# A banded convolution and soft mixture of experts on one core: convolutions and channel turns as two 64-row tiles

## The chip, the cores and the metric

The kernel runs on one core of a Trainium2 chip, in one launch. The metric is the device time of that launch in microseconds (us), measured three times before the change. A profile of one more execution gives the durations and waits used below. The engines are called as in the profile: PE (TensorE, the matrix engine; PEld are its weight loads), DVE (VectorE), ACT (ScalarE), POOL (GpSimd) and SP (SyncE, which here only starts DMAs).

## What is computed

A causal convolution over seven positions, whose taps are a softmax of `weight_gen`, one set for each token and head; then a soft mixture of experts over all 28672 tokens. All is float32.

```python
w = softmax(weight_gen, axis=-1)                     # (8, 3584, 8 heads, 7 taps)
out = einsum('bshk,bskhg->bshg', w, x_unf)           # x_unf: 7 shifted copies of x
x = out.reshape(28672, 192)
logits = x @ phi                                     # 32 slots
d = softmax over the tokens (axis 0) of logits
slot_input = (d.T @ x).reshape(8, 4, 192)            # 8 experts, 4 slots each
h = maximum(slot_input[e] @ w1[e], 0); slot_out[e] = h @ w2[e]
c = softmax over the slots (axis 1) of logits
return c @ slot_out
```

## The kernel before

**Tiling.** A group is 104 tokens: four blocks of 26. A batch has 35 groups, so there are 280 groups, 140 pairs and 70 slots of two pairs. `x` comes by supergroups of five groups into a ring `xbd` (a view of `big`): the rows of a block's 32 positions, four times on the partitions, once for each of four heads, in block-diagonal form, so that one contraction over 128 partitions does four heads at once. The off-diagonal parts are zeroed once (`clear`, L354) and only the diagonal is loaded (`loadx`, L152, four DMAs of 120 KB).

**Taps.** A chunk is 8 groups of taps, one chunk for two slots, 35 in all. A chunk goes through `tap_top` (DVE maximum), `tap_sub` (POOL), `tap_exp` (ACT), `tap_sum` (three folds on POOL), `tap_inv` (DVE reciprocal), `tap_mul` (POOL, writes the taps on diagonals of `wide`) and `tap_turn` (DVE transpose of 32 by 32 blocks), which gives a `band`, the stationary operand of the convolution.

**Loop.** For each pair, `conv` (L222) does 16 matmuls: 2 groups, 2 halves of the heads, 4 blocks, each of 128 rows by 26 weight columns with 96 columns streamed, into one PSUM bank `cv`, the block choosing the 32 partitions written. `conv_out` (L235) copies 384 columns to `tm` on ACT. `xpose` (L241) turns a pair's channels to the partitions with three transposes of 122 rows by 128 columns into `pt`, and `xpose_out` (L252) copies 312 columns to `cm` on ACT. For every unit of 8 pairs (four slots), `logits` (L271) multiplies by `phi`, `top`, `newmax`, `newmax_out`, `dexp`, `dturn` keep a running maximum over the tokens and its exponentials, and `dispatch` (L334) adds `d.T @ x`; `fade` and `rescale` correct the sum for a new maximum. `soft` (L75) does the row softmax `c` of a half batch in seven steps over DVE, POOL and ACT; the first 13 (`EARLY`) of 16 halves run inside the loop.

**Order.** The queues are filled in an order that the program works out: every piece is an `op` with its engine, an assumed cost, what it reads and writes and sometimes a due time, and `model` places them. PE and SP keep the order in which the loop writes them; DVE, ACT and POOL are sorted. In a slot, PE does two `conv`, with `newmax` between them where it is due, then `logits` where due, two `xpose`, and `dispatch` where due.

**Rings before the change.** Four `x` buffers of four zeroed quarter heads, four `taps`, one `wide`, three `band`, two `tm`, four `cv` (a bank each), two `pt` (a bank each), one bank each for the logits `ls` and the accumulator `acb`. After the loop, the experts' network runs on `accS` (the accumulated sum), and the output is 49 evictions from PSUM into parts of `big` and as many DMAs.

Of the kernel before, what the change touches and what calls it, by code (L numbers as in the profile page):

```python
# [42 lines left out]
def conv_soft_moe(ctx, tc, xh, wh, phi, w1a, w1b, w2, out):  # L43
# [96 lines left out]
    A.copy(xbd[:, 0, 2], zero.to_broadcast([128, NBC * GW]))  # L140
    V.memset(xbd[:, 0, 3], 0.0)
    for t in taps:
        V.memset(t[:, :, KT], EPS)
# [19 lines left out]
    def seven(t):  # L163
        return t.rearrange("p b k j -> p b j k")

    def each(t, n):
        return t.unsqueeze(2).to_broadcast([128, n, KT, T])

    def tap_top(c, b=ALL):
        n = b.stop - b.start  # L170
        m = tops[c, b.start] = pa.tile([128, CH, T], F32, tag="top", name=f"top{c}_{b.start}")[:, 0:n]
        V.tensor_reduce(out=m, in_=seven(taps[c % NTAP][:, b, 0:KT]), axis=AX.X, op=ALU.max)  # L172
# [6 lines left out]
    def tap_exp(c, b=ALL):  # L179
        t = taps[c % NTAP][:, b, 0:KT]  # L180
        A.activation(t, t, AF.Exp)  # L181

    def tap_sum(c, b=ALL, eng=None):
        n = b.stop - b.start
        m = tsums[c, b.start] = pa.tile([128, CH, T], F32, tag="sum", name=f"sum{c}_{b.start}")[:, 0:n]
        t, s = taps[c % NTAP][:, b], fold[:, b]
        if eng is None:
            V.tensor_reduce(out=m, in_=seven(t), axis=AX.X, op=ALU.add)
            return
        eng.tensor_tensor(out=s, in0=t[:, :, 0:4], in1=t[:, :, 4:8], op=ALU.add)  # L190
        eng.tensor_tensor(out=s[:, :, 0:2], in0=s[:, :, 0:2], in1=s[:, :, 2:4], op=ALU.add)
        eng.tensor_tensor(out=m, in0=s[:, :, 0], in1=s[:, :, 1], op=ALU.add)  # L192
# [5 lines left out]
    def tap_mul(c, b=ALL, eng=G):  # L198
# [3 lines left out]
        w = wide[:, b]  # L202
        dst = bass.AP(w.tensor, w.offset, [w.ap[0], [T * 32, n], [1, KT], [33, T]])
        eng.tensor_tensor(out=dst, in0=taps[c % NTAP][:, b, 0:KT],  # L204
                          in1=each(m, n), op=ALU.mult)

    def tap_turn(c, b=ALL):

        V.transpose(bands[c % NBAND][:, b].rearrange("p b j l -> p (b j l)"),  # L209
                    wide[:, b].rearrange("p b j -> p (b j)"))  # L210
# [11 lines left out]
    def conv(p):  # L222
        cv = cvs[p % NCV]
        for par in range(2):
            g = 2 * p + par
            t = g // SGG
            for c in range(2):
                for blk in range(4):
                    o = 4 * GW * (2 * par + (c ^ par))
                    i, b = ((4 * (g % m) + blk) * 2 + c for m in (4, SGG))  # L230
                    P.matmul(cv[32 * blk : 32 * blk + T, o : o + 4 * GW],  # L231
                             bands[g // 8 % NBAND][:, g // 4 % CH, :, i],
                             xbd[:, t % NXS, :, b * GW : (b + 1) * GW], start=True, stop=True)

    def conv_out(p, copy=A.copy):  # L235
        u, pr = unit(p)
        copy(tms[u % NTM][:, pr, 1 : 2 * D + 1], cvs[p % NCV][:, 0 : 2 * D])  # L237
# [3 lines left out]
    def xpose(p):  # L241
        u, pr = unit(p)
# [3 lines left out]
        pt = ps_t.tile([128, 4, 128], F32, tag="pt", name=f"pt{p}")[:, 0:3]  # L246
        pts[p] = pt
        for i in range(3):
            P.transpose(pt[:, i, 0:TR], tm[0:TR, pr, 1 + 128 * i : 129 + 128 * i],  # L249
                        ident[0:TR, 0:TR])  # L250

    def xpose_out(p, copy=A.copy):  # L252
        u, pr = unit(p)
        copy(cms[u][:, pr].rearrange("p i b j -> p (i b) j"),  # L254
             pts.pop(p).rearrange("p i (b j) -> p (i b) j", j=32)[:, :, 0:T])

# [46 lines left out]
    def newmax_out(u):  # L303
        negm[u] = pa.tile([128, 1], F32, tag="nm", name=f"nm{u}", bufs=3)
        V.tensor_reduce(out=negm[u], in_=pm[:, 0 : 4 + (u > 0)], axis=AX.X, op=ALU.min)
# [27 lines left out]
    def dispatch(u, lo=0, hi=2 * UP):  # L333
# [3 lines left out]
        if lo == 0:  # L337
            acs[u] = (acb if u < final else cvs[sum(UNITS[u]) % NCV])[:, 0 : D + 1]
# [571 lines left out]
```

## Time and profile before

| | us |
|---|---|
| median of 3 runs | 321.17 (320.27 to 323.70) |
| the profiled execution | 320.73 |
| its span, first to last instruction | 319.0 |
| mean granted clock of PE | 0.925 |
| PE busy | 272.7 |
| DVE busy | 220.8 |
| ACT busy | 185.5 |
| POOL busy | 154.7 |
| DMA, 70.06 MB | 220 GB/s over the span |

An engine's busy time is the sum of its instructions, over stages with different limits: an opening without steady work for PE, the loop, the experts' network, and an output stage in which PE has little to do. Float32 matmuls show as two records each (2240 matmuls of the convolution, 4480 records), transposes as one. In a row of the timeline, the first two numbers are the start and the length from the first record's start to the last one's end, and xN counts the records merged; the bracket at the end is idle time of that engine and what ended it.

### The profile page before, as it was taken

How to read it: one execution, taken by the hardware profiler on the slowest of the kernel's cores; microseconds unless marked ns; L12 is line 12 of the kernel's file. 1: busy time of each engine (PE TensorE's matmuls, PEld its weight loads, DVE VectorE, ACT ScalarE, POOL GpSimd, SP SyncE). 2: the span in 40 equal slices, each digit the busy share in tenths (PEclk: the TensorE clock that was granted, in tenths of full speed). 3: DMA queues.
4: the chain of work that ended last, by engine and by line, in shares of the span. 5: the costliest groups of instructions: out<-in, count | busy, mean ns of one | idle time of the engine just before them, and what ended most of it. 6: DMA issues, size and time to landing. Idle time of an engine off the chain costs nothing.

```text
span 319.0 us, 15477 instructions
## 1 busy us (share of the span) xinstructions
PE 272.7 (85%) x6816; PEld 210.1 (66%) x6816; DVE 220.8 (69%) x366; ACT 185.5 (58%) x425; POOL 154.7 (49%) x236
## 2 busy tenths in 40 slices
PE   6656999999999999999999999999989987789100
PEld 6645888788788888887888887878768721223000
DVE  5826669788688787788796895797436689964200
ACT  5553666777678677687677667676642266534200
POOL 5867553756857757687639665486015500000000
PEclk9587999999999999999999999999999999985555
DMA  5267467758765767677667756763990069999994
GB/s 169 57 176 217 134 196 212 209 165 234 182 208 159 217 187 209 184 225 201 193 188 211 221 162 190 206 189 85 392 386 8 4 233 402 400 400 402 400 401 172
DMA packets 32146, 70.06 MB, mean 220 GB/s; under 512 B 5456, under 2 KB 14800, under 8 KB 32080
## 3 DMA queue, kind: packets, MB, share of 16 engines
q1 hardware_dynamic: 32080, 69.08, 67.7%
q8 instruction: 53, 0.87, 1.2%
q14 instruction: 13, 0.11, 0.1%
HBM read 46.70 MB, written 22.36 MB: 217 GB/s over the span
## 4 chain that ended last, share of the span: by engine, by line
PE 62%; DMA 13%; DVE 10%; POOL 4%; issue 3%; ACT 2%; SPq 0%; ACTq 0%; DVEq 0%; POOLq 0%
PE cv L231 28%; PE pt L249 14%; DMA out<-big 8%; PE ls L278 7%; PE acb L342 7%; DMA taps<-wh 5%; DVE band L209 2%; DVE big L808 2%; PE hpb L732 2%; PE so L753 2%; DVE top L172 1%; POOL big L358 1%; DVE cT L445 1%; POOL wide L204 1%; ACT big L808 1%
## 5 line engine op out<-in xcount | busy, mean ns | idle before, releaser
L231 PE MATMUL cv<-big,band 128*26 128x96 f32 x4480 | 117.5, 255 | 10.8 <-POOL si L190 4.4
L231 PEld LDWEIGHTS cv<-big,band 128*26 128x26 f32 x4480 | 103.3, 132 | 22.2 <-issue 9.5
L237 ACT COPY tm<-cv 128x384 f32<-128x384 f32 x140 | 67.2, 482 | 43.0 <-PE cv L231 40.0
L209 DVE STREAM_TRANSPOSE band<-wide 128x1664 f32<-128x1664 f32 (+1 forms) x37 | 66.6, 1801 | 3.4 <-POOL wide L204 3.3
L254 ACT COPY cm<-pt 128x312 f32<-128x312 f32 x140 | 53.9, 424 | 18.4 <-PE pt L249 18.3
L249 PE MATMUL pt<-ident,tm 122*128 122x122 f32 x420 | 60.0, 279 | 2.7 <-ACT cm L254 2.7
L249 PEld LDWEIGHTS pt<-ident,tm 122*128 122x128 f32 x420 | 43.8, 142 | 15.4 <-issue 5.8
L176 POOL TENSOR_TENSOR taps<-taps,top 128x364 f32<-128x364 f32 (+1 forms) x35 | 31.1, 892 | 29.0 <-DVE top L172 29.0
L204 POOL TENSOR_TENSOR wide<-taps,sum 128x364 f32<-128x364 f32 (+1 forms) x35 | 31.4, 899 | 19.6 <-DVE sum L196 17.5
L801 PE MATMUL po<-cT,so 32*128 32x468 f32 (+3 forms) x256 | 33.7, 667 | 7.1 <-DVE big L808 6.7
L172 DVE TENSOR_REDUCE top<-taps 128x52 f32<-128x364 f32 (+1 forms) x36 | 29.6, 821 | 11.7 <-DMA taps<-wh 11.7
L808 ACT COPY big<-po 128x936 f32<-128x936 f32 (+2 forms) x25 | 22.4, 902 | 24.7 <-DMA out<-big 14.6
L808 DVE COPY big<-po 128x884 f32<-128x884 f32 (+2 forms) x24 | 25.3, 1066 | 10.2 <-DMA out<-big 9.0
L801 PEld LDWEIGHTS po<-cT,so 32*128 32x128 f32 (+1 forms) x256 | 10.4, 175 | 29.3 <-DVE big L808 24.4
L278 PE MATMUL ls<-cm,phi_sb 128*32 128x208 f32 (+1 forms) x576 | 29.2, 334 | 0.4 <-issue 0.4
L190 POOL TENSOR_TENSOR si<-taps 128x208 f32<-128x208 f32 x34 | 21.6, 635 | 14.1 <-ACT taps L181 13.8
L196 DVE RECIPROCAL sum<-sum 128x52 f32<-128x52 f32 (+1 forms) x36 | 16.4, 456 | 15.3 <-POOL sum L192 15.1
L342 PE MATMUL acb<-tm,dt 128*32 128x193 f32 x536 | 26.0, 330 | 0.0
L181 ACT ACTIVATE taps<-taps 128x364 f32<-128x364 f32 (+1 forms) x36 | 18.3, 507 | 8.3 <-POOL taps L176 7.4
L278 PEld LDWEIGHTS ls<-cm,phi_sb 128*32 128x32 f32 x576 | 18.7, 109 | 5.5 <-issue 1.1
L93 POOL TENSOR_TENSOR LT<-LT,sm 128x576 f32<-128x576 f32 (+1 forms) x16 | 18.2, 1135 | 7.4 <-DVE sm L91 7.4
L81 POOL TENSOR_TENSOR LT<-LT,rm 128x576 f32<-128x576 f32 (+1 forms) x16 | 18.1, 1135 | 5.1 <-DVE rm L79 4.8
(106 smaller groups left out, 245.2 us busy)
## 6 DMA issues: line engine op xcount, KB each, us to landing
big<-xh SPq DMA_DIRECT2D x224, 120.0 KB, 3.3
out<-big SPq DMA_DIRECT2D x23, 468.0 KB, 6.4
out<-big SPq DMA_DIRECT2D x24, 442.0 KB, 6.5
taps<-wh SPq DMA_DIRECT2D x35, 182.0 KB, 4.0
big<-w SPq DMA_DIRECT2D x8, 768.0 KB, 8.2
w1a_sb<-w1a SPq DMA_DIRECT2D x16, 256.0 KB, 3.6
w1b_sb<-w1b SPq DMA_DIRECT2D x8, 256.0 KB, 3.8
out<-big SPq DMA_DIRECT2D x2, 234.0 KB, 2.3
```

The source lines that it names most:

```text
L172: V.tensor_reduce(out=m, in_=seven(taps[c % NTAP][:, b, 0:KT]), axis=AX.X, op=ALU.max)
L176: eng.tensor_tensor(out=t, in0=t, in1=each(tops.pop((c, b.start)), b.stop - b.start), op=ALU.subtract)
L204: eng.tensor_tensor(out=dst, in0=taps[c % NTAP][:, b, 0:KT], in1=each(m, n), op=ALU.mult)
L209: V.transpose(bands[c % NBAND][:, b].rearrange("p b j l -> p (b j l)"), wide[:, b].rearrange("p b j -> p (b j)"))
L231: P.matmul(cv[32 * blk : 32 * blk + T, o : o + 4 * GW], bands[g // 8 % NBAND][:, g // 4 % CH, :, i], xbd[:, t % NXS, :, b * GW : (b + 1) * ...
L237: copy(tms[u % NTM][:, pr, 1 : 2 * D + 1], cvs[p % NCV][:, 0 : 2 * D])
L249: P.transpose(pt[:, i, 0:TR], tm[0:TR, pr, 1 + 128 * i : 129 + 128 * i], ident[0:TR, 0:TR])
L254: copy(cms[u][:, pr].rearrange("p i b j -> p (i b) j"), pts.pop(p).rearrange("p i (b j) -> p (i b) j", j=32)[:, :, 0:T])
L278: P.matmul(lp[32 * blk : 32 * blk + 32, 0:n, par, 0:T], phi_sb[:, 2 * par + i, :], cm[:, 0:n, 1 if i else 2 * par, blk, :], start=(i == 0) ...
L342: P.matmul(ac[32 * q : 32 * q + 32], dt[:, g, :], tm[:, g // 2, o : o + D + 1], start=(g < 4), stop=(g + 4 >= 2 * n))
L801: P.matmul(po[dst : dst + hi - lo, at, 0 : n * T], so[32 * q : 32 * q + 32, lo:hi], cT[32 * q : 32 * q + 32, g0 : g0 + n, 0:T], start=True ...
L808: (V.tensor_copy if done[1] % 2 else A.copy)(ot.rearrange("p (q c) -> p q c", c=n * T), po[:, 0 : len(qs), 0 : n * T])
```

## The change

The contraction of 128 rows, of which a quarter is of use to each head, becomes two of 64 rows.

- **Convolution.** `conv(k)` now does a whole slot: 64 matmuls instead of 32, each of 64 rows by 26 weight columns with 48 columns streamed. The upper and the lower 64 rows (`z`) write to a PSUM bank each. `conv_out` copies both pairs, 768 columns in two banks, with one ACT instruction. There are two such `cv` (four banks in all, as before).
- **Channel turn.** `xpose(k)` does 12 transposes of 58 rows by 128 columns for a slot, the two `z` into a bank each; one `pt` of two banks instead of two of one. `xpose_out` copies 624 columns at once.
- **x ring.** Half the columns per buffer (two instead of four halves to clear), six buffers instead of four. The loads keep their size.
- **Taps.** Six `taps`, two `exps` (the exponentials get their own tile), two `wide`. The innermost axis is now the seven taps of a token, in `wh` and on the chip, where it was the 26 tokens.
- **Order.** `xpose(k - 1)` follows `conv(k)`; `newmax` comes after it; `dispatch` is a slot later, the last on PE in its slot, and that slot's `conv_out` is put behind it. The fifth column of `newmax` is prepared on POOL (`keepmax`). The planner's costs are others.
- **Opening.** Two taps loads first, chunk 2's maximum, subtraction and exponential ahead of the planned part, and constants, identity and the last clears inside the planned part.
- **Row softmax and experts.** `EARLY` is 8: five more half batches are done in the output stage, one step after an eviction. The loads of `w2` are started expert by expert as the ring's buffers come free.

```diff
-WARM = 9, 5
+WARM = 9, 14
-EARLY = 13
+EARLY = 8
-TR = 3 * 32 + T
+TR = 32 + T
-    NXS = 4
-    XB = 4 * NBC * GW
+    NXS = 6
+    XB = 2 * NBC * GW
-    NTM, NCV, NTAP, NBAND = 2, 4, 4, 3
+    NTM, NCV, NTAP, NEX, NW, NBAND = 2, 2, 6, 2, 2, 3
...
+    def conv(k):
+        cv = cvs[k % NCV]
+        for pp in range(2):
+            for par in range(2):
+                g = 4 * k + 2 * pp + par
+                t = g // SGG
+                for c in range(2):
+                    o = 2 * GW * (4 * pp + 2 * par + (c ^ par))
+                    for z in range(2):
+                        r = slice(64 * z, 64 * z + 64)
+                        for blk in range(4):
+                            i, b = ((4 * (g % m) + blk) * 2 + c for m in (4, SGG))
+                            P.matmul(cv[32 * blk : 32 * blk + T, z, o : o + 2 * GW],
+                                     bands[g // 8 % NBAND][r, g // 4 % CH, :, i],
+                                     xbd[r, t % NXS, :, b * GW : (b + 1) * GW], start=True, stop=True)
...
+    def xpose(k):
...
+        pt = pts[k] = ps_t.tile([128, 2, 512], F32, tag="pt", name=f"pt{k}")
+        for pp in range(2):
+            for i in range(3):
+                for z in range(2):
+                    r = slice(64 * z, 64 * z + TR)
+                    at = 64 * (3 * pp + i)
+                    P.transpose(pt[:, z, at : at + TR],
+                                tm[r, pr + pp, 1 + 128 * i : 129 + 128 * i], ident[r, r])
...
     for k in range(1, SLOTS):
+        op(TE, CONV, conv_reads(k), [("cv", k % NCV)], conv, k)
+        if k not in dispatched:
+            op(AC, 0.8, [], [("cv", k % NCV), tm_of(k)], conv_out, k)
...
+        op(TE, TURN, [tm_of(k - 1), "ident"], ["pt"], xpose, k - 1)
+        op(AC, 0.68, [], ["pt", cm_of(k - 1)], xpose_out, k - 1)
...
+    rest = sorted((4 * i + k, h, k) for i, h in enumerate(range(EARLY + 3, 2 * B)) for k in range(7))
...
             leave(po, STEPS[st][1], qs)
+            while rest and rest[0][0] <= done[1]:
+                soft(pc, *rest.pop(0)[1:])
```

What this does to the queues, in rows of the built programs (operation, output, inputs, shape of the output, count). PE before, around the first unit's end: `cv` and `pt` are PSUM tiles, `ls` the logits, `acb` the accumulator.

```order
L278 MATMUL ls<-cm_305,phi_sb 32x8x26 x16
L249 MATMUL pt_548<-ident,tm_93 128x122 x3
L249 MATMUL pt_556<-ident,tm_93 128x122 x3
L231 MATMUL cv_95<-big,band_89 26x96 x16
L301 MATMUL acb<-mq,sel_125 32x4 x4
L231 MATMUL cv_96<-big,band_89 26x96 x16
L249 MATMUL pt_609<-ident,tm_93 128x122 x3
L249 MATMUL pt_614<-ident,tm_93 128x122 x3
L231 MATMUL cv_97<-big,band_89 26x96 x16
L231 MATMUL cv_98<-big,band_89 26x96 x16
L249 MATMUL pt_662<-ident,tm_93 128x122 x3
L249 MATMUL pt_671<-ident,tm_93 128x122 x3
```

The `dispatch` (16 matmuls of 32x193) stands right behind these. The same place on PE after the change:

```order
L279 MATMUL ls<-cm_356,phi_sb 32x8x26 x16
L251 MATMUL pt_753<-ident,tm_98 128x58 x12
L228 MATMUL cv_100<-big,band_94 26x48 x64
L251 MATMUL pt_844<-ident,tm_98 128x58 x12
L302 MATMUL acb<-mq,sel_124 32x4 x4
L228 MATMUL cv_101<-big,band_94 26x48 x64
L251 MATMUL pt_933<-ident,tm_98 128x58 x12
L228 MATMUL cv_100<-big,band_95 26x48 x64
L251 MATMUL pt_1022<-ident,tm_98 128x58 x12
L345 MATMUL acb<-tm_97,dt_951 32x193 x16
```

Twice as many matmuls of half the columns; `newmax` (L302) moved from between two convolutions to between a turn and a convolution, and `dispatch` (L345) a slot back. The logits, `newmax` and `dispatch` keep their 128 rows, so they now stand between instructions of another tile shape.

ACT in the same slots before (`cv` to `tm`, `pt` to `cm`, and `dexp` on `dd`):

```order
L237 COPY tm_93<-cv_95 128x384
L237 COPY tm_93<-cv_96 128x384
L254 COPY cm_547<-pt_609 128x312
L311 ACTIVATE dd<-ls,nm_635 128x16x26
L254 COPY cm_547<-pt_614 128x312
L237 COPY tm_93<-cv_97 128x384
L254 COPY cm_547<-pt_662 128x312
L237 COPY tm_93<-cv_98 128x384
```

And after:

```order
L235 COPY tm_98<-cv_100 128x2x2x4x48
L256 COPY cm_752<-pt_844 128x2x6x52
L314 ACTIVATE dd<-ls,nm_926 128x16x26
L235 COPY tm_98<-cv_101 128x2x2x4x48
L256 COPY cm_752<-pt_933 128x2x6x52
L176 ACTIVATE exps_91<-taps_89 128x52x7
L256 COPY cm_752<-pt_1022 128x2x6x52
L235 COPY tm_97<-cv_100 128x2x2x4x48
```

One eviction of each kind for a slot; the last two rows are the slot with a `dispatch`, where `conv_out` comes behind `xpose_out`.

POOL in the opening before, up to the product for the third band (`band_91`):

```order
L204 TENSOR_TENSOR wide<-taps_85,sum_0_171 128x7x26 x2
L358 MEMSET big 128x960 x5
L420 MEMSET selE_126 128x128
L421 MEMSET dd 128x384
L422 MEMSET qneg 128x4
L423 MEMSET q_128 128x1
L424 MEMSET q_128 32x1
L426 MEMSET qneg 32x1 x4
L176 TENSOR_TENSOR taps_86<-taps_86,top_0_278 128x2x182
L176 TENSOR_TENSOR taps_87<-taps_87,top_0_301 128x2x182
L190 TENSOR_TENSOR si<-taps_86 128x208
```

And after, up to the third band's product (L199, `wide_92`):

```order
L199 TENSOR_TENSOR wide_93<-exps_91,sum_0_189 128x26x7
L172 TENSOR_TENSOR taps_86<-taps_86,top_0_196 128x364
masks.py:197 MEMSET ident 128x128
masks.py:199 AFFINE_SELECT ident<-ident 128x128
L361 MEMSET big 128x960
L185 TENSOR_TENSOR si<-exps_90 128x208
L186 TENSOR_TENSOR si<-si 128x52x2
L187 TENSOR_TENSOR sum_0_437<-si 128x52
L361 MEMSET big 128x960
L199 TENSOR_TENSOR wide_92<-exps_90,sum_0_437 128x2x26x7
```

Chunk 2's subtraction stood behind five clears and the constants, and its sum behind chunk 3's subtraction; now the sum stands behind one clear, the constants come later, and chunk 3 is behind it.

More of the change, by code (lines that the diff above doesn't have):

```diff
@@ L139, in conv_soft_moe @@
     G.memset(xbd[:, 0, 1], 0.0)
[L140 to L143, printed above, removed]
+    for t in exps:
+        V.memset(t[:, :, :, KT], EPS)
     V.memset(eps, EPS)
@@ L220, in unit, with conv_out @@
         return next((u, p - p0) for u, (p0, n) in enumerate(UNITS) if p < p0 + n)
[L222 to L237, printed above, removed]
+    def conv(k):
[13 more added lines that the diff above has]
+                                     xbd[r, t % NXS, :, b * GW : (b + 1) * GW], start=True, stop=True)
+    def conv_out(k, copy=A.copy):
+        u, pr = unit(2 * k)
+        tm = tms[u % NTM][:, pr : pr + 2, 1 : 2 * D + 1]
+        copy(tm.rearrange("p a (s z w) -> p z a s w", s=4, z=2),
+             cvs[k % NCV][:, :, 0 : 2 * D].rearrange("p z (a s w) -> p z a s w", a=2, s=4))
     cms, pts = {}, {}
-    def xpose(p):
-        u, pr = unit(p)
+    def xpose(k):
+        u, pr = unit(2 * k)
         tm = tms[u % NTM]
@@ L245, in xpose, with xpose_out @@
             cms[u] = pa.tile([128, UP, 3, 4, T], F32, tag="cm", name=f"cm{u}", bufs=1)
[L246 to L255, printed above, removed]
+        pt = pts[k] = ps_t.tile([128, 2, 512], F32, tag="pt", name=f"pt{k}")
[6 more added lines that the diff above has]
+                                tm[r, pr + pp, 1 + 128 * i : 129 + 128 * i], ident[r, r])
+    def xpose_out(k, copy=A.copy):
+        u, pr = unit(2 * k)
+        copy(cms[u][:, pr : pr + 2].rearrange("p a i (z b) j -> p z (a i) b j", z=2),
+             pts.pop(k)[:, :, 0 : 6 * 64].rearrange("p z (s b j) -> p z s b j", b=2, j=32)[:, :, :, :, 0:T])
     DUP = (NG - 1) * GT - LAST
@@ L337, in dispatch @@
         if lo == 0:
-            acs[u] = (acb if u < final else cvs[sum(UNITS[u]) % NCV])[:, 0 : D + 1]
+            acs[u] = acb[:, 0 : D + 1] if u < final else cvs[SLOTS % NCV][:, 0, 0 : D + 1]
         ac = acs[u]
@@ L406, in conv_soft_moe @@
     conv_out(0)
-    clear_cv(3)
-    clear(2, 1, A)
-    loadx(2)
-    for h in range(4):
-        clear(3, h, G)
-    loadx(3)
-    loadw(3)
-    SY.dma_start(phi_sb, phi)
-    conv(1)
-    conv_out(1)
     for t in tms:
@@ new lines, in cm_of, with cm_all @@
+    def cm_of(k):
+        return ("cm", unit(2 * k)[1])
+    def cm_all(u):
+        return [("cm", pr) for pr in range(0, UNITS[u][1], 2)]
+    VE, AC, PO, TE, SP = "VE", "AC", "PO", "TE", "SP"
+    for lag, what in ((0.0, x_of(1)), (1.0, x_of(2)), (3.0, x_of(3)), (0.0, ("w", 1)),
+                       (0.0, ("w", 2)), (2.0, ("w", 3)), (0.8, ("band", 0)),
+                      (3.5, ("band", 1)), (2.5, ("e", 0))):
+        op(SP, 0.0, [], [what], lambda: None, late=lag)
+    op(PO, 0.5, [], ["ident"], make_identity, nc, ident)
@@ L496, in conv_soft_moe @@
+    for i in range(4, NXS):
+        op(PO, 0.9, [], [x_of(i)], clear, i, 1, G)
+        op(AC, 1.0, [], [x_of(i)], clear, i, 0, A)
+        op(SP, 2.0, [], [x_of(i)], loadx, i, late=3.0)
+    op(SP, 0.3, [], [], SY.dma_start, phi_sb, phi)
+    op(PO, 1.2, [], ["dd", "sel4"], setup)
+    op(VE, 0.8, ["sel4"], ["ls", "acb"], consts)
     for q in range(4):
-        op(AC, 0.6 - 0.3 * (q % 2), [], ["sel4"], sums, q)
-    for lag, what in ((1.0, x_of(1)), (3.0, x_of(2)), (7.0, x_of(3)), (0.0, ("w", 1)),
-                       (0.0, ("w", 2)), (0.0, ("w", 3)), (1.0, ("band", 0))):
-        op(SP, 0.0, [], [what], lambda: None, late=lag)
+        op(AC, 0.6 - 0.3 * (q % 2), ["ident"], ["sel4"], sums, q)
@@ L512, in conv_soft_moe @@
+        if c > 2:
+            op(VE, 0.56, [w], [("top", c % 2)], tap_top, c)
+            op(PO, 0.88, [("top", c % 2)], [w], tap_sub, c)
+            op(AC, 0.5, [w], [e], tap_exp, c)
+        op(PO, 1.15, [e], [("sum", c % 2), "fold"], tap_sum, c, ALL, G)
+        op(VE, 0.45, [], [("sum", c % 2)], tap_inv, c)
+        op(PO, 0.89, [("sum", c % 2), e], [("wide", c % NW)], tap_mul, c)
+        op(VE, 1.86, [("wide", c % NW)], [("band", c % NBAND)], tap_turn, c)
     softs = {}
```

228 lines of the change are left out of this document (113 added, 115 removed).

## The prediction

> **What bounds the kernel now.** I read the page's busy shares and slices first, then busy time by stretches, then PE's timeline over a unit, then the groups by line.
>
> ```profile
> span 319.0 us, 15477 instructions
> ...
> PEclk9587999999999999999999999999999999985555
> DMA  5267467758765767677667756763990069999994
> ...
> 29.60:232.64 203.04, 200.65 (x5806) 167.60 (x5807) 158.98 (x265) 140.91 (x350) 124.93 (x182) 0.99 0.69 200
> 262.00:319.00 57.00, 28.01 (x212) 8.34 (x208) 27.42 (x30) 18.29 (x20) 0.00 (x0) 0.70 0.94 368
> ...
> 262.00:275.00 13.00, 9.35 (x100) 2.58 (x96) 13.00 (x16) 8.23 (x9) 0.00 (x0) 1.00 1.02 402
> ```
>
> The rows of stretches give the length, then the busy time of PE, PEld, DVE, ACT and POOL, the granted clock, the DMA share and GB/s. Three stages: an opening until 29.60; the loop until 232.64, where PE is busy 200.65 of 203.04 us and nothing else is over 79%; and an output stage from before 262 in which the DMA engines are full (1.02, 402 GB/s) and the other engines have room. So time in the loop is PE's to give, time in the output stage is not. The profiled execution took 320.73 us, its span 319.0; the median of the runs is 321.17, 0.44 above. I forecast against 320.73.
>
> ```profile
> 111.77 0.84 PE L249 MATMUL pt<-ident,tm 122*128 122x122 f32 x6
> 112.54 1.56 PE L231 MATMUL cv<-big,band 128*26 128x96 f32 x64
> 114.03 0.85 PE L249 MATMUL pt<-ident,tm 122*128 122x122 f32 x6
> 114.80 1.60 PE L342 MATMUL acb<-tm,dt 128*32 128x193 f32 x32
> 116.13 1.59 PE L231 MATMUL cv<-big,band 128*26 128x96 f32 x64
> ...
> 120.55 1.63 PE L278 MATMUL ls<-cm,phi_sb 128*32 128x208 f32 x32
> 122.11 0.84 PE L249 MATMUL pt<-ident,tm 122*128 122x122 f32 x6
> ...
> 123.59 0.23 PE L301 MATMUL acb<-mq,sel 128*32 128x5 f32 x8
> ...
> L231 PE MATMUL cv<-big,band 128*26 128x96 f32 x4480 | 117.5, 255 | 10.8 <-POOL si L190 4.4
> ```
>
> Start to start, a slot's turns take 0.77 us (111.77 to 112.54), its convolutions 1.49 (112.54 to 114.03), `dispatch` 1.33, the logits 1.56. A unit is 4 x (0.77 + 1.49) + 1.33 + 1.56 + about 0.1 for `newmax` = 12.0 us, and the 66 slots from 29.60 on are 16.5 units, 198 us; the other 5 of the 203 are waits.
>
> Inside a convolution, 64 records start within 1.56 - 0.255 us, so one every 20.7 ns. Four blocks share the columns, so one column tile has a record every 83 ns: 96 columns, 0.87 ns each. 64 x 20.7 ns is 1.33; the remaining 0.16 of the 1.49 is the edge, entering and leaving a run of matmuls. A turn streams 122 columns, 0.106 us at that rate, six times 0.64; its edge is 0.13.
>
> **Convolution.** 32 matmuls of 96 columns become 64 of 48: 128 records a slot. If the two row tiles run side by side, eight tiles share the work, and two paces bound it.
>
> ```profile
> L231 PEld LDWEIGHTS cv<-big,band 128*26 128x26 f32 x4480 | 103.3, 132 | 22.2 <-issue 9.5
> ...
> L301 PEld LDWEIGHTS acb<-mq,sel 128*32 128x32 f32 x144 | 3.8, 110 | 1.2 <-DVE mq L287 0.9
> ...
> L301 PE MATMUL acb<-mq,sel 128*32 128x5 f32 (+1 forms) x144 | 4.2, 174 | 0.3 <-DVE mq L287 0.2
> ...
> 261.04 1.02 PE L801 MATMUL po<-cT,so 32*128 32x442 f32 x8 [0.39 <-DVE big L808]
> ```
>
> Do row tiles run side by side? The output stage has tiles of 32 rows and all 128 columns, each with its own bank: eight records of 442 columns, 0.385 us each at 0.87 ns, 3.1 us one after another, in 1.02. They do, at least four at once. How fast can records start? `newmax` streams only five columns: eight records, 0.174 us each, within 0.23, so seven intervals in 0.056, 8.0 ns each, weight loads included; with the rounding of the row 6.6 to 9.4. I take 7.5, the lower side, since its two records of one tile also wait for each other: 128 x 7.5 = 0.96, with the edge 1.12 us. The lower bound is one tile's own work: 16 records, each at least 48 x 0.87 = 42 ns of columns, and about 51 if its weights set it (two rounds of `newmax` in 0.056, so 28 ns, and the band's strided columns load 132 - 110 = 22 ns longer): 0.82 + 0.16 = 0.98. The upper is 8.7 ns, 1.27. So 1.49 to 1.12, 66 slots: -24.4 us (-14.5 to -33.7).
>
> **Turns.** Six records of 122 columns become twelve of 58 in two row tiles. Bounds: only columns count, 6 x 0.050 + 0.13 = 0.43; or a record keeps its pace because the 128 weight columns set it, 0.77. L801 loads 128 weight columns in four row tiles at once, so nearer the low end: 0.52. -0.25 x 66 = -16.5 us (-22.4 to 0).
>
> **Edges.** Before, `newmax` and `dispatch` had the convolution's shape and stood next to it, the logits behind it. Now each stands between 64-row tiles, which makes three more changes of shape a unit. The nearest row is the convolution's edge next to the turn, 0.16 us: 3 x 16.5 x 0.16 = +7.9 us (0 to 7.9; an edge is never a gain). [...]
>
> **ACT.** Evictions merge:
>
> ```profile
> L237 ACT COPY tm<-cv 128x384 f32<-128x384 f32 x140 | 67.2, 482 | 43.0 <-PE cv L231 40.0
> L254 ACT COPY cm<-pt 128x312 f32<-128x312 f32 x140 | 53.9, 424 | 18.4 <-PE pt L249 18.3
> L181 ACT ACTIVATE taps<-taps 128x364 f32<-128x364 f32 (+1 forms) x36 | 18.3, 507 | 8.3 <-POOL taps L176 7.4
> L311 ACT ACTIVATE dd<-ls,nm 128x416 f32<-128x416 f32 (+1 forms) x18 | 11.0, 612 | 3.0 <-DVE nm L305 3.0
> L329 ACT ACTIVATE al<-nm,nm 128x1 f32<-128x1 f32 x17 | 5.2, 303 | 0.0
> ```
>
> 72 columns more cost 58 ns, 0.8 ns a column, so 768 columns take 0.79 us and 624 take 0.67: 1.46 a slot instead of 1.81. But there is one `pt` now: `xpose(k)` waits until `xpose_out(k - 1)`, which stands on ACT behind `conv_out(k)`. From the end of `conv(k)`, ACT needs 0.79 + 0.67 and three handovers; PE gets there after a turn and a convolution, 1.64. So a plain slot has under 0.2 us of room: what ACT puts between (0.51 twice, 0.61 and 0.30 a unit, 0.48 a slot) is waited for, while slots with logits or `dispatch` hide it. A fifth of it, 0.1 a slot, is my value: +6.6, and the 5 us of old waits, on rings that are now deeper, go: +1.6 together (-5 to +28, all 0.5 a slot).
>
> **DVE, POOL, row softmax.**
>
> ```profile
> L172 DVE TENSOR_REDUCE top<-taps 128x52 f32<-128x364 f32 (+1 forms) x36 | 29.6, 821 | 11.7 <-DMA taps<-wh 11.7
> L79 DVE TENSOR_REDUCE rm<-LT 128x18 f32<-128x576 f32 (+1 forms) x16 | 11.4, 718 | 0.1
> L87 DVE TENSOR_REDUCE sm<-LT 128x18 f32<-128x576 f32 (+1 forms) x16 | 11.4, 714 | 4.8 <-ACT LT L84 4.8
> L81 POOL TENSOR_TENSOR LT<-LT,rm 128x576 f32<-128x576 f32 (+1 forms) x16 | 18.1, 1135 | 5.1 <-DVE rm L79 4.8
> ```
>
> Five halves leave the loop: 5 x (0.72 + 0.71) = 7.2 us of DVE, 5 x 2 x 1.135 = 11.4 of POOL. The maximum reads 364 values with a stride, 0.82 us; L79 reads 576 in a row in 0.72, so the new layout makes it 0.46 to 0.82, 0 to 11 us for the 31 chunks. DVE has 141 to 152 us of work left for a loop that PE makes about 172 us, 82 to 88%: a neighbour, no bound. In the loop this is worth nothing by itself. In the output stage DVE is busy 27.42 of 57 us, POOL not at all, behind full DMAs: 0 (up to +7.2).
>
> **Opening.** The loop starts when the third band is there:
>
> ```profile
> 23.78 0.89 POOL L176 TENSOR_TENSOR taps<-taps,top 128x364 f32<-128x364 f32 x1 [2.92 <-DVE top L172]
> ...
> 29.60 2.79 PE L231 MATMUL cv<-big,band 128*26 128x96 f32 x64 [2.87 <-DVE band L209]
> ...
> L209 DVE STREAM_TRANSPOSE band<-wide 128x1664 f32<-128x1664 f32 (+1 forms) x37 | 66.6, 1801 | 3.4 <-POOL wide L204 3.3
> ...
> L358 POOL MEMSET big<- 128x960 f32 x8 | 6.9, 900 | 0.0
> L381 POOL MEMSET wide<- 128x832 f32 x1 | 0.8, 791 | 0.0
> L176 POOL TENSOR_TENSOR taps<-taps,top 128x364 f32<-128x364 f32 (+1 forms) x35 | 31.1, 892 | 29.0 <-DVE top L172 29.0
> L190 POOL TENSOR_TENSOR si<-taps 128x208 f32<-128x208 f32 x34 | 21.6, 635 | 14.1 <-ACT taps L181 13.8
> L191 POOL TENSOR_TENSOR si<-si 128x104 f32<-128x104 f32 x34 | 13.9, 408 | 2.7
> L192 POOL TENSOR_TENSOR sum<-si 128x52 f32<-128x52 f32 x34 | 9.4, 277 | 2.7
> L204 POOL TENSOR_TENSOR wide<-taps,sum 128x364 f32<-128x364 f32 (+1 forms) x35 | 31.4, 899 | 19.6 <-DVE sum L196 17.5
> ```
>
> Before, POOL sat behind chunk 3's late taps until 23.78. After, POOL's queue up to the third product is six clears 5.4, three `wide` clears 2.4, subtractions 2.3, sums 3.5, products 2.0, identity 0.5: 16.1, from about 1 us on and with about 1 of waits for ACT and DVE 18; the transpose 1.9 makes it 20. PE's first four slots, then two bands of about 5 us on POOL each, keep just ahead: -9.5 us (-5 to -10).
>
> **Past the loop.** Before, one expert of `w2` came last; now three do, but their first reader stands well behind:
>
> ```profile
> 232.64 0.84 PE L249 MATMUL pt<-ident,tm 122*128 122x122 f32 x6
> ...
> 248.59 1.48 PE L753 MATMUL so<-big,hT 128*32 128x192 f32 x32
> ```
>
> 16 us cover 2.4 MB, about 6 us at 402 GB/s: 0. Nothing else moves there. Sum: -24.4 - 16.5 + 7.9 + 1.6 - 9.5 = -40.9; 320.7 - 40.9 = 280 us. Its own range is 268 to 291.
>
> **Rivals.**
> - *ACT sets the slot.* The one `pt` and the longer evictions make PE wait for ACT's other 0.5 us a slot, all of it or, caught up every second slot, half, 0.25: +11.5 to +28 in place of +1.6, 290 to 306, 298. For it: the 1.46 against 1.64 above, and 40 us of ACT's idle time ended by PE now, so they already alternate. Against: half the slots have 1.3 to 1.6 us of slack.
> - *PE at its lower bounds.* Convolution 0.98, turn 0.43, edges hidden, old waits gone: -33.7 - 22.4 - 5 - 9.5, 250 us; half-way there, about 262. Against: at 250 the loop is 142 us, no more than DVE's own work of 141 to 152; half-way, DVE is at 90% or more.
> - *The row tiles don't overlap* (slower). A convolution is then 32 rounds of 51 ns, 1.63 + 0.16 = 1.79, +0.30 a slot or +19.8, and the turns gain nothing: +7.9 + 1.6 - 9.5 besides, 341 us. It decides from 1.74 us a convolution on, 12.3 ns a record. For it: no row shows 64-row tiles of 32 columns. Against: L801.
> - *Records have a floor.* If 20.7 ns is the least between two records however few the columns, a convolution is 128 x 20.7 ns + 0.16 = 2.81, +1.32 a slot, +87; with the other terms 391 us. Against: the 8.0 ns of `newmax`. [...]
>
> **How the numbers follow.** The forecast 0.60, ACT 0.18, PE's bounds 0.14, rows not overlapping 0.03, a floor 0.02, and 0.03 that what is won in the loop comes back elsewhere, no change. About 1% is what a measurement of this kernel can tell from none. Faster by over 1%: 0.60 + 0.18 + 0.14 = 0.92; same 0.03; slower 0.05. The range goes from 262, half-way to PE's bounds, to 300, past the middle of ACT's: it leaves out half of PE's case, about a third of ACT's and those that don't gain, 2 in 10.
>
> **What the profile would show.** Right: L228 x128 in about 1.0 us, start to start 1.1; L251 x12 in 0.5; PE over 90% busy from 20 us on; a unit in about 10.2 us; the output stage full of DMA some 41 us earlier. Edges: gaps of 0.1 to 0.2 beside L279, L302, L345. ACT: L251 waiting for ACT cm in plain slots. Wrong: L228 x128 over 1.7 us, L251 x12 over 0.77, DVE over 90% with PE waiting for `band`, the first L228 of the fifth slot after 25 us, or DMAs below 400 GB/s in the output stage for want of evictions.

## The result, and the profile after

The changed kernel takes 444.66 us (median of 4 runs, 443.59 to 448.99) against 321.20 (320.27 to 323.70) for the kernel before on the same chip: 1.385 times as long, 95% interval 1.373 to 1.397. The forecast was 280 us.

Where the 123.6 us between the two spans lie, from the starts of the fifth slot's first convolution matmul, of the last convolution matmul and of the first output matmul:

| stage | before | after | difference |
|---|---|---|---|
| until the fifth slot | 29.6 | 23.5 | -6.1 |
| fifth slot to last convolution | 202.9 | 330.9 | +128.0 |
| last convolution to first output matmul | 23.4 | 24.3 | +0.9 |
| output | 63.1 | 63.9 | +0.8 |

So it is the loop. These are lines of the changed kernel's page. The line that begins with "PE 63%" gives the shares of the span in the chain of work that ended last; a group's row ends with its idle time and what ended it:

```profile
span 442.6 us, 25264 instructions
PE 322.5 (73%) x11734; PEld 232.2 (52%) x11734; DVE 207.4 (47%) x346; ACT 173.1 (39%) x284; POOL 149.9 (34%) x254
PEclk9656686995877858595967667586858599865965
q8 instruction: 92, 1.51, 1.5%
PE 63%; issue 21%; DVE 4%; POOL 4%; DMA 2%; ACT 1%; SPq 1%; DVEq 0%; POOLq 0%; ACTq 0%
L228 PE MATMUL cv<-big,band 64*26 64x48 f32 x8960 | 132.9, 253 | 75.5 <-issue 75.4
L235 ACT COPY tm<-cv 128x768 f32<-128x768 f32 x70 | 57.0, 815 | 122.0 <-PE cv L228 120.6
L256 ACT COPY cm<-pt 128x624 f32<-128x624 f32 x70 | 47.7, 681 | 85.5 <-PE pt L251 85.4
```

PE is idle for a quarter of the span, and what would feed it is idle for longer still: ACT waits for PE, not PE for ACT. The convolution's 75 us of idle time are ended by "issue": nothing that the profile shows as a semaphore or a transfer was waited for. The granted clock alternates between full and half (1.00 and 0.50 in its records, 0.71 on average over the loop). Busy time over the loop, columns as in the prediction:

```profile
23.50:354.60 331.10, 246.42 (x10416) 189.47 (x10414) 139.30 (x229) 127.00 (x216) 109.60 (x188) 0.71 0.44 129
```

PE went through 10416 + 10414 = 20830 instructions in 331.1 us, 62.9 a microsecond. The loop before, by the row in the prediction, took 5806 + 5807 in 203.04 us, 57.2 a microsecond. The rate rises by a tenth only, while the columns behind each matmul of the convolution halve: that is the first sign. PE's timeline over nearly three slots of the changed kernel is the second. A bracket that ends in "issue" is called a stop from here on:

```profile
200.57 0.80 PE L228 MATMUL cv<-big,band 64*26 64x48 f32 x41 [2.23 <-issue]
201.30 0.89 PE L251 MATMUL pt<-ident,tm 58*128 58x58 f32 x12
202.13 1.20 PE L228 MATMUL cv<-big,band 64*26 64x48 f32 x74
204.61 0.93 PE L228 MATMUL cv<-big,band 64*26 64x48 f32 x54 [1.29 <-issue]
205.48 0.89 PE L251 MATMUL pt<-ident,tm 58*128 58x58 f32 x12
206.30 2.80 PE L345 MATMUL acb<-tm,dt 128*32 128x193 f32 x32
209.03 1.64 PE L228 MATMUL cv<-big,band 64*26 64x48 f32 x128
210.60 1.60 PE L279 MATMUL ls<-cm,phi_sb 128*32 128x208 f32 x29
213.10 0.54 PE L279 MATMUL ls<-cm,phi_sb 128*32 128x208 f32 x3 [0.90 <-issue]
213.57 0.58 PE L251 MATMUL pt<-ident,tm 58*128 58x58 f32 x12
```

Count the records between stops: from 200.57 to 204.61, 41 + 12 + 74 = 127; each comes with a weight load, so 254 instructions, in 4.04 us. From 204.61 to 213.10, 54 + 12 + 32 + 128 + 29 = 255, so 510 instructions, twice 255, in 8.49 us. The stops stand in the middle of a convolution or of the logits, wherever the count falls. And the queue of instructions moved 92 packets, 1.51 MB, for 23468 records: 16 KB and 255 records a packet. In the kernel before the same queue and the one stop that the prediction's rows passed over read:

```profile
q8 instruction: 53, 0.87, 1.2%
```

```profile
118.43 1.20 PE L231 MATMUL cv<-big,band 128*26 128x96 f32 x43
119.97 0.80 PE L231 MATMUL cv<-big,band 128*26 128x96 f32 x21 [0.34 <-issue]
```

13632 records in 53 packets, 257 each, and a small stop inside a convolution. There were six stops in that loop, 2.0 us in all; the changed kernel's loop has 62, 84.6 us.

**Theory.** PE's instructions arrive in blocks of about 256 (126 to 128 records, each with a weight load, between two stops of the changed loop, or two or three times as many; 16 KB a packet), and a block takes about 3.95 us (packets start every 3.9 us in the changed loop, median). A matmul of the convolution is four instructions (two records, two weight loads: 8960 of each for 4480 matmuls), a transpose of the turn two (840 and 840 for 840). A unit had 4 x (32 x 4 + 6 x 2) + 144 = 704, 2.75 blocks, 10.9 us of supply under 12.0 us of work: just fed. It now has 4 x (64 x 4 + 12 x 2) + 144 = 1264, 4.94 blocks, 19.5 us. **Rivals:** the matmuls' own pace in 64-row tiles (shape, two banks, edges); the halved clock; the order, ring or evictions.

The packets' times in the kept traces bear on it directly. Each of the 62 stops in the changed loop ends 1.11 to 1.63 us (median 1.41) after the end of a packet of the instruction queue, and the six of the loop before 1.24 to 1.48 us after one. The next packet starts 1.34 us (median; 1.03 at the least) after a stop has ended and takes 1.07 us (median). Together 1.34 + 1.07 + 1.41 = 3.8 us: in these stops PE went on 1.11 to 1.63 us after a packet had come, and the next packet started only after that, 1.03 us later or more.

### The profile page after: what moved, and what is told of

It reads as the page before. It is cut to its first block, busy times and chain, and to the rows that moved or that the text cites. A ratio compares the mean times of both kernels' runs of the same rounds, so it can differ in the third digit from the quotient of the medians.

```text
span 442.6 us, 25264 instructions
## 1 busy us (share of the span) xinstructions
PE 322.5 (73%) x11734; PEld 232.2 (52%) x11734; DVE 207.4 (47%) x346; ACT 173.1 (39%) x284; POOL 149.9 (34%) x254
## 3 DMA queue, kind: packets, MB, share of 16 engines
q8 instruction: 92, 1.51, 1.5%
## 4 chain that ended last, share of the span: by engine, by line
PE 63%; issue 21%; DVE 4%; POOL 4%; DMA 2%; ACT 1%; SPq 1%; DVEq 0%; POOLq 0%; ACTq 0%
PE cv L228 28%; PE pt L251 11%; PE acb L345 10%; PE ls L279 8%; PE po L824 2%; DVE big L831 2%; DMA out<-big 2%; PE hpb L755 1%; PE so L776 1%; DVE cT L451 1%; POOL LT L81 1%; PE acb L302 1%; POOL big L361 1%; DVE rm L79 1%; SPq L833 1%
## 5 line engine op out<-in xcount | busy, mean ns | idle before, releaser
L228 PE MATMUL cv<-big,band 64*26 64x48 f32 x8960 | 132.9, 253 | 75.5 <-issue 75.4
L228 PEld LDWEIGHTS cv<-big,band 64*26 64x26 f32 x8960 | 113.3, 139 | 94.7 <-issue 91.1
L235 ACT COPY tm<-cv 128x768 f32<-128x768 f32 x70 | 57.0, 815 | 122.0 <-PE cv L228 120.6
L256 ACT COPY cm<-pt 128x624 f32<-128x624 f32 x70 | 47.7, 681 | 85.5 <-PE pt L251 85.4
L251 PE MATMUL pt<-ident,tm 58*128 58x58 f32 x840 | 55.2, 282 | 10.3 <-issue 7.9
L251 PEld LDWEIGHTS pt<-ident,tm 58*128 58x128 f32 x840 | 43.4, 183 | 22.6 <-issue 14.1
L185 POOL TENSOR_TENSOR si<-exps 128x208 f32<-128x208 f32 (+1 forms) x35 | 21.7, 621 | 82.8 <-ACT exps L176 82.7
L345 PE MATMUL acb<-tm,dt 128*32 128x193 f32 x536 | 45.8, 516 | 0.0
L199 POOL TENSOR_TENSOR wide<-exps,sum 128x364 f32<-128x364 f32 (+1 forms) x35 | 28.1, 805 | 28.6 <-DVE sum L191 28.6
L345 PEld LDWEIGHTS acb<-tm,dt 128*32 128x32 f32 x536 | 22.7, 164 | 14.0
```

The source lines that it names most:

```text
L199: eng.tensor_tensor(out=dst, in0=exps[c % NEX][:, b, :, 0:KT], in1=each(m, n), op=ALU.mult)
L228: P.matmul(cv[32 * blk : 32 * blk + T, z, o : o + 2 * GW], bands[g // 8 % NBAND][r, g // 4 % CH, :, i], xbd[r, t % NXS, :, b * GW : (b + 1 ...
L235: copy(tm.rearrange("p a (s z w) -> p z a s w", s=4, z=2), cvs[k % NCV][:, :, 0 : 2 * D].rearrange("p z (a s w) -> p z a s w", a=2, s=4))
L251: P.transpose(pt[:, z, at : at + TR], tm[r, pr + pp, 1 + 128 * i : 129 + 128 * i], ident[r, r])
L256: copy(cms[u][:, pr : pr + 2].rearrange("p a i (z b) j -> p z (a i) b j", z=2), pts.pop(k)[:, :, 0 : 6 * 64].rearrange("p z (s b j) -> p z ...
L345: P.matmul(ac[32 * q : 32 * q + 32], dt[:, g, :], tm[:, g // 2, o : o + D + 1], start=(g < 4), stop=(g + 4 >= 2 * n))
```

## The experiments

**The rest of the change alone.** Convolution and turn back on 128 rows, all else as changed (but three full x buffers, which is what fits, with the clears and the planner's costs to match).

```diff
-    NXS = 6
-    XB = 2 * NBC * GW
+    NXS = 3
+    XB = 4 * NBC * GW
...
-                    for z in range(2):
-                        r = slice(64 * z, 64 * z + 64)
-                        for blk in range(4):
...
+                    for blk in range(4):
...
+                        P.matmul(cv[32 * blk : 32 * blk + T, pp, o : o + 4 * GW],
+                                 bands[g // 8 % NBAND][:, g // 4 % CH, :, i],
+                                 xbd[:, t % NXS, :, b * GW : (b + 1) * GW], start=True, stop=True)
...
+                P.transpose(pt[:, pp, 128 * i : 128 * i + TR],
+                            tm[0:TR, pr + pp, 1 + 128 * i : 129 + 128 * i], ident[0:TR, 0:TR])
```

> The changed kernel with the convolution and the turn put back to 128-row tiles (32 matmuls of 96 columns and 6 turns of 122 rows for two pairs); the one eviction for two pairs, the order, the tap buffers and the opening stay as changed; the x ring is three full buffers. Instruction supply (PE gets 256 instructions in no less than about 3.95 us): 704 PE instructions in a unit, 10.9 us of supply, below the 12.0 us of PE's work, so no stops; 305 us (295 to 320), by the earlier opening and fewer edges between shapes. Rival, that the order, the ring or the merged evictions cost the time: above 345.

317.39 us, 0.987 of before (0.979 to 0.996): inside the supply's range, though 12 us above its 305, and far from the rival's 345. The whole loss is in the two row-tiled parts; the rest gains a little. PE's longest waits in it:

```profile
PE po L820 <- DVE big L827: 4.8, 8, 1.4
PE pt L246 <- POOL si L187: 2.9, 1, 2.9
PE cv L228 <- DMA big<-xh: 2.4, 1, 2.4
PE ls L274 <- issue: 1.7, 1, 1.7
...
PE pt L246 <- ACT cm L251: 1.1, 2, 0.6
```

**The convolution on 128 rows, the turn in row tiles.** As above, without the last two lines of the diff.

> As the kernel above, but with the turn in two 64-row tiles as changed; only the convolution is back on 128 rows. Instruction supply: 752 PE instructions in a unit, 11.6 us of supply against about 12 us of work, so few stops: 312 us (300 to 330). Rival, that 64-row tiles or the eviction across two banks are slow in themselves, whatever the number of instructions: the turn keeps half of the loss, 345 or more.

322.84 us, 1.003 of before (0.998 to 1.009): inside the supply's range of 300 to 330, though 11 us above its 312 and not with "few stops". Its timeline shows a turn that is faster and a gain that is lost again:

```profile
151.79 0.52 PE L249 MATMUL pt<-ident,tm 58*128 58x58 f32 x10 [0.54 <-issue]
152.24 1.55 PE L228 MATMUL cv<-big,band 128*26 128x96 f32 x64
153.72 0.58 PE L249 MATMUL pt<-ident,tm 58*128 58x58 f32 x12
154.23 0.24 PE L300 MATMUL acb<-mq,sel 128*32 128x5 f32 x8
154.31 0.87 PE L228 MATMUL cv<-big,band 128*26 128x96 f32 x32
156.10 0.89 PE L228 MATMUL cv<-big,band 128*26 128x96 f32 x32 [0.92 <-issue]
```

A turn takes 0.51 us start to start (153.72 to 154.23; the median of all turns at full clock without a stop is 0.51 too) instead of 0.77, 1.04 us less a unit. But 752 instructions need 11.7 us at the 3.98 a block that the kernel with all matmuls in two shows (in the table below), and the loop has 24 stops, 17.6 us in all, in place of 6 and 2.0; a unit took 12.37 us.

**Empty instructions on PE** (before, with four behind each convolution matmul).

```diff
+                    for _ in range(4):
+                        P.nop("x", nofuse=True)
```

> The kernel before with four empty instructions on PE behind each convolution matmul: 8960 more, 1216 PE instructions in a unit (the changed kernel has 1264), and not one matmul, byte or wait changed. Instruction supply: 4.75 blocks of 256 at 3.95 us is 18.8 us a unit against 12.0, so 16.5 units give about +111: 425 to 445 us, with PE stopped after each 254 to 256 instructions. Rival, that an instruction costs only its issue (half of the 10.9 ns between two records of the changed kernel's bursts): 8960 x 5.5 ns is 49 us: 370. Rival, that the tile's shape is the cause: 321 to 335.

860.62 us: a miss for all three, and no test. An empty instruction took (860.62 - 321.55) / 8960 = 60 ns on PE, so blocks came 9.3 us apart (median) and the supply was not what bound it.

**Twice the instructions, nothing else.** The kernel before, each convolution matmul issued as two of half the columns; then the same for every other group only (`n = 1 + par`).

```diff
-                    P.matmul(cv[32 * blk : 32 * blk + T, o : o + 4 * GW],
-                             bands[g // 8 % NBAND][:, g // 4 % CH, :, i],
-                             xbd[:, t % NXS, :, b * GW : (b + 1) * GW], start=True, stop=True)
+                    n = 2
+                    for h in range(n):
+                        w = 4 * GW // n
+                        P.matmul(cv[32 * blk : 32 * blk + T, o + w * h : o + w * h + w],
+                                 bands[g // 8 % NBAND][:, g // 4 % CH, :, i],
+                                 xbd[:, t % NXS, 4 // n * h : 4 // n * (h + 1), b * GW : (b + 1) * GW],
+                                 start=True, stop=True)
```

> The kernel before with each convolution matmul of 96 columns issued as two of 48, over the same 128 rows into the same bank: the same result, no row tiles, nothing else moved. 1216 PE instructions in a unit. Instruction supply: 4.75 blocks of 256 at 3.95 us is 18.8 us a unit in place of 12.07, 321 + 16.5 x 6.7 = 431 us (415 to 445), with stops after 254 to 256 instructions and a unit of 18 to 19.5 us. Rival, that 64-row tiles, the two banks or the order lose the time: 128 records of between 10.7 ns (the changed kernel's with 8 columns) and 16 ns (its upper tile alone) are 1.37 to 2.05 us in place of 1.43: 317 to 362 us.

> As the kernel above, but only every other group's matmuls are issued in two: 960 PE instructions in a unit. Instruction supply: 14.8 us a unit, 321 + 16.5 x 2.75 = 366 us (355 to 380). Rival as above: 319 to 342 us.

430.64 and 376.95 us, against 431 and 366 by the supply and at most 362 and 342 by the rival. This is the decisive pair: 128-row tiles, one bank, the old order, and a loss of 106 and 52 us against the kernel before on the same chip (324.67). Not all of it is supply. In the first, a convolution that met no stop took 2.05 to 2.34 us at full clock (median of four 2.17) in place of 1.43, a little over the 2.05 at the top of the rival's range:

```profile
146.31 2.12 PE L234 MATMUL cv<-big,band 128*26 128x48 f32 x128
148.36 0.84 PE L253 MATMUL pt<-ident,tm 122*128 122x122 f32 x6
```

Over 66 slots, 0.74 us more each would have cost 49 us by itself. But that pace alone ends at about 374 us, far below 430.64; the rest came with 62 stops, 55 us of idle time (in the second kernel, 41 stops and 27.9 us). These are lines from the page of the first, then its group of `dispatch` (min, median and max of a record), its loop and its timeline:

```profile
PEclk9779999999999799999999999999999899999555
...
q8 instruction: 88, 1.44, 1.5%
```

```profile
L346 PE MATMUL acb<-tm,dt x536: 323/327/530, 48.3 to 347.1; 128*32 128x193 f32 x179
```

```profile
29.70:342.60 312.90, 255.51 (x10030) 220.71 (x10030) 160.75 (x265) 143.69 (x350) 125.29 (x182) 0.98 0.47 138
```

```profile
201.68 1.47 PE L234 MATMUL cv<-big,band 128*26 128x48 f32 x86 [0.38 <-issue]
203.07 0.85 PE L253 MATMUL pt<-ident,tm 122*128 122x122 f32 x6
203.85 0.77 PE L234 MATMUL cv<-big,band 128*26 128x48 f32 x35
206.18 1.44 PE L234 MATMUL cv<-big,band 128*26 128x48 f32 x87 [1.55 <-issue]
```

86 + 6 + 35 = 127 records between stops, 20060 instructions in 312.9 us, 64.1 a microsecond, as in the changed kernel. And the clock was granted in full, 0.98 over the loop, with a median `dispatch` record of 327 ns, where the changed kernel had 0.71 and

```profile
L345 PE MATMUL acb<-tm,dt x536: 326/528/529, 48.8 to 359.8; 128*32 128x193 f32 x179
```

So the halved clock isn't needed for the loss. The changed kernel has both, the stops and the half clock. PE's busy time in that loop also rose, by 45.8 us (200.65 to 246.42), in part at the half clock; how much of this would only have become longer stops at full clock wasn't taken apart. At `dispatch` itself the half clock seems to cost little, since a slow `dispatch` (2.73 us start to start at 206.30, 1.33 at full clock in the kernel before) leaves the next block time to arrive (204.61 to 213.10 above: two blocks without a stop).

**Less work, the same instructions.** The changed kernel with 8 of 48 columns; with the weights side by side instead of 128 bytes apart; with x loaded for six buffers only.

```diff
-                            P.matmul(cv[32 * blk : 32 * blk + T, z, o : o + 2 * GW],
+                            P.matmul(cv[32 * blk : 32 * blk + T, z, o : o + 8],
...
-                                     xbd[r, t % NXS, :, b * GW : (b + 1) * GW], start=True, stop=True)
+                                     xbd[r, t % NXS, :, b * GW : b * GW + 4], start=True, stop=True)
```

```diff
-                                     bands[g // 8 % NBAND][r, g // 4 % CH, :, i],
+                                     bands[g // 8 % NBAND][r, g // 4 % CH, i % T, 0:T],
```

```diff
-                    op(SP, 2.0, [], [x_of(t)], loadx, t + NXS, late=3.0)
+                    pass
```

> The changed kernel, each convolution matmul with 8 of its 48 columns, so that five sixths of the convolution's output are not computed; the number of instructions is the same. Instruction supply: 1264 instructions in a unit as before the cut, 19.5 us, so 435 to 450 us, no change. Rival, that the matmuls' own pace is the cause: of the 48 columns' time five sixths go; with 16.5 units of four convolutions of 1.57 us at least 40 us less, 400 or below.

> The changed kernel with the convolution's 26 weight columns taken side by side in place of 128 bytes apart, so the output is not the reference's. Instruction supply: the time stays, 435 to 450 us, since the number of instructions does. Within a burst: if the weights' spacing sets the 80 ns that 8 records take, a convolution that meets no stop takes about 0.8 to 1.0 us in place of 1.57; if it does not, 1.57 stays.

> The changed kernel that loads x for its first six buffers alone and convolves these again and again, so the output is not the reference's; the PE instructions are the same. If the time of a block's refill is a wait in the DMA queues behind the loads of x: blocks of 256 at 3.5 us or less in place of 3.95, 408 us or less. If it is the refill's own latency: no change, 435 to 448 us.

440.10, 443.70 and 436.54 us. Against 444.66, whose own runs reach from 443.59 to 448.99, five sixths of the convolution's columns were worth 4.6 us, the weights' spacing 1, and the loads of x 8; these are single runs on other chips, so the small differences are not settled. The refill's time is hardly one of DMA traffic: without the loads (DMA share 0.19 between 24 and 345 us, in place of 0.44) the packets still start 3.8 us apart (median), though one packet itself takes 1.1. The first of the three also gives the pace of records that no stop delays:

```profile
206.64 1.44 PE L228 MATMUL cv<-big,band 64*26 64x8 f32 x128
208.01 1.65 PE L279 MATMUL ls<-cm,phi_sb 128*32 128x208 f32 x29
```

128 records of 8 columns take 1.37 us, 10.7 ns each. With 48 columns it is 1.57 in the row above (209.03 to 210.60) and 1.49 at full clock (median of 4). So a fed convolution in two row tiles takes what it took before. The weights' spacing is a small part of it: side by side it is 1.35 at full clock (median of 11), not 0.8 to 1.0.

**Fewer instructions.** The changed kernel without the lower rows' matmuls, in all pairs (`range(1)`) or every other (`range(2 - pp)`), so that half and a quarter of the convolution's output are missing.

```diff
-                    for z in range(2):
+                    for z in range(1):
```

> The changed kernel without the convolution matmuls of the lower 64 rows, so that half of the convolution's output is not computed. 752 PE instructions in a unit in place of 1264. Instruction supply: 2.94 blocks of 256 at 3.95 us is 11.6 us a unit in place of 19.4 measured, above the 9.7 us that PE has to do (four of 0.8 and 0.83, and 3.2): 445 - 16.5 x 7.8 = 316 us (305 to 330), still with stops after 254 to 256 instructions. Rival, that the matmuls' own pace is the cause: 64 records of 10.9 ns and their waits go in each of 66 slots, 0.8 us each: 392 us.

> The changed kernel without the lower rows' convolution matmuls in every other pair, so that a quarter of the convolution's output is not computed: 1008 PE instructions in a unit. Instruction supply: 15.55 us a unit, 445 - 16.5 x 3.85 = 381 us (370 to 392). Rival, the matmuls' own pace: 418 us.

326.74 and 390.64 us: within the supply's ranges, at their upper ends, and far from the rival's 392 and 418. In the first, a convolution in the upper tile alone:

```profile
210.02 1.11 PE L228 MATMUL cv<-big,band 64*26 64x48 f32 x64
211.06 0.45 PE L251 MATMUL pt<-ident,tm 58*128 58x58 f32 x7
```

1.04 us for 64 records. Two tiles take 1.49, not 2.08: they do run side by side, only not twice as fast.

**The turn on 128 rows, the convolution in row tiles.** The two transpose lines of the first diff on the changed kernel.

> The changed kernel with only the turn put back to 128-row tiles; the convolution stays in two 64-row tiles. 1216 PE instructions in a unit in place of 1264. Instruction supply: 0.19 of a block less, 0.74 us a unit: 445 - 12 = 433 us (425 to 440). Rival, that the turn in row tiles is a cause of its own beside the supply (0.83 us in place of 0.77, or more): below 420.

434.82 us, by the supply 433 (425 to 440), by the rival below 420.

**Both parts on 128 rows, with 13 half batches of the row softmax in the loop** (`EARLY = 13`).

> The kernel with both parts on 128-row tiles and the changed order (317 us), with 13 soft steps ahead of the output as in the kernel before in place of 8. If the later soft steps cost time behind the loop (24.4 us between the last convolution and the first output matmul against 23.4): 315 to 317 us; if they are hidden under the output's transfers: 317 to 319.

315.55 us, 0.972 of before (0.969 to 0.974): faster than both kernels of this study. Against 8 half batches the two ratios to the kernel before, 0.972 and 0.987, point to a gain, but where it would lie isn't shown: the two ran on different chips, and the stretch behind the loop is no shorter (24.7 against 24.4 us).

All together, with the median distance between the starts of successive `dispatch` groups as the unit. The first three and the last row were run four times or more, the others once; all runs of the kernel before lie between 318.8 and 325.2 us:

| kernel | PE instructions a unit | unit, us | us for 256 | time, us |
|---|---|---|---|---|
| before | 704 | 12.07 | 4.39 | 321.2 |
| both on 128 rows | 704 | 11.87 | 4.32 | 317.4 |
| convolution on 128 rows | 752 | 12.37 | 4.21 | 322.8 |
| upper rows only | 752 | 12.96 | 4.41 | 326.7 |
| before, every other group in two | 960 | 15.79 | 4.21 | 377.0 |
| three quarters | 1008 | 16.43 | 4.17 | 390.6 |
| before, all in two | 1216 | 18.89 | 3.98 | 430.6 |
| turn on 128 rows | 1216 | 19.43 | 4.09 | 434.8 |
| 8 columns | 1264 | 19.19 | 3.89 | 440.1 |
| x not reloaded | 1264 | 19.14 | 3.88 | 436.5 |
| weights side by side | 1264 | 19.64 | 3.98 | 443.7 |
| changed | 1264 | 19.87 | 4.02 | 444.7 |

In these twelve kernels the time follows the instructions, whatever their shapes; among kernels of the same number the order is not settled. The column of 256 falls towards 3.9 as the supply binds more of the unit. The kernel with empty instructions is not in the table: there PE was slower than the supply.

## Why the prediction was wrong

- **The step that failed** is the convolution's "two paces bound it". Both paces were those of the tiles, columns and weight loads; that doubling the matmuls doubles PE's instructions stood nowhere in the sum. `newmax` showed how fast eight records start, and this was carried to 128 records a slot and 1264 instructions a unit, for which the blocks aren't there: a unit took 19.87 us in place of the about 10.2 of the prediction, one block every 4.0 us. The rows to see it were in the profile before: 53 packets of 16 KB, 57 instructions a microsecond, and a stop for "issue" inside a convolution. Going from one block to the next cost little in the kernel before (57 instructions a microsecond, 2.0 us of stops), but not in the changed one (63, and 84.6 us).
- **The convolution's own size** was wrong too: 7.5 ns a record, an estimate from `newmax`, 1.12 us, against 10.7 ns even with 8 columns and 1.49 us at full clock. Fed, it would have won nothing. That the records have a floor was a rival with 0.02, at 20.7 ns; the direction was right, the place of the loss was not. From 48 to 8 columns a convolution without a stop went only from 1.57 to 1.37 us (209.03 and 206.64 above, the same place of the loop). Why `newmax` starts its records closer, I can't say. The weight loads, 167.60 of 203.04 us in the prediction's row, are 83%, over the 79% that the prediction gives as the most for anything but PE.
- **The turn** was right in size: 0.52 forecast, 0.51 at full clock. At half clock it is 0.82 (median of those without a stop in the changed kernel). Its -16.5 us didn't reach the total: with it alone, on the 128-row convolution, the stops grew by 15.6 us and the loop got no shorter.
- **The edges'** +7.9 was an estimate, and no run shows that a change of shape costs 0.16 us. What the rows above show is a turn of one length, whichever shape follows: at half clock 0.83 us before a convolution (201.30) and 0.82 before `dispatch` (205.48), at full clock 0.51 before `newmax` (153.72), the median of all turns. The other edges can't be seen between the stops, and weren't measured apart.
- **ACT.** The evictions take 0.815 and 0.681 us, forecast 0.79 and 0.67. That the one `pt` makes PE wait did not show: with both parts on 128 rows, PE waited 1.1 us in all for `xpose_out`. But a slot took 2.97 us there (a quarter of 11.87), and no run reached the forecast's 2.55, so whether the rival would have come true at that pace isn't shown.
- **Opening.** The fifth slot starts at 23.5 us, not 20: -6.1 for -9.5 (and 24.6, -5.0, with 128-row tiles).
- **DVE, row softmax, `w2`.** The tap maximum takes 0.50 us, inside 0.46 to 0.82. What lies behind the loop was put at 0 and cost 1.7.
- **The signs of a miss** that the prediction named don't include the cause. A fed convolution stayed under the 1.7 us (the row above at 209.03 reads 1.64); a turn went over 0.77, but at half clock only; PE over 90% busy, which was to show it right, is what failed (246 of 331 us).

Not settled: what happens in the 1.3 us before and the 1.4 us after the 1.1 us of a packet.

## What to carry to other kernels

Count the instructions of the engine that bounds the kernel, weight loads and float32's second records among them, and divide by 256, the block that came here every 3.9 us at best (table). The packets of the instruction queue and the rate over the loop told how far a kernel was from its supply: this one, at 57 instructions a microsecond where the six with 1216 or more a unit got 62.6 to 64.5, had no room for twice as many, however well they run side by side. Each split into smaller matmuls spent from it: 1216 instructions a unit in place of 704 took 430.64 us in place of 324.67. Idle time that "issue" ends inside a run of independent matmuls, every 126 to 128 records or a multiple of that, was the mark of it.

## What the hardware showed that was not expected

- PE's instructions came at 62.6 to 64.5 a microsecond, from the fifth slot to the last convolution, in all six kernels with 1216 to 1264 a unit, with stops of 0.89 to 1.53 us on average, although within a burst one was issued every 5.4 ns (256 in 1.37 us, with 8 columns).
- In the loops of these six, every stop ended 1.07 to 1.64 us after the end of a packet of the instruction queue.
- An empty instruction on PE took 60 ns, some ten times the 5.4 ns of a matmul or weight load within a burst.
- Two 64-row tiles with 32-column blocks ran side by side, 1.49 us for what one does in 1.04 each, yet no faster than 128-row tiles of twice the columns (1.43 to 1.49). The same 128 rows in matmuls of half the columns took 2.17.
- With such stops the granted clock went to half for stretches of mostly 10.2 or 13.7 us in the changed kernel (0.71 over the loop, stops of 1.36 us on average), but hardly in the one with the matmuls cut in two (0.98, 0.89 us). What decides it wasn't tried.
